# A branch-prefetch hint on VectorE ahead of each slot's choice between two block forms

## The chip, the cores and the metric

The kernel runs on one core of a Trainium2 chip. The metric is device time in microseconds (us) of one execution. The kernel before takes 819.59 us, the median of three runs (819.03, 819.59 and 821.61 us).

## The reference

Three layers follow one another on 3072 tokens of 512 features: a retention attention with a decaying state, and two mixture-of-experts layers in which each token goes to one of eight experts. Cut to the second kind of layer:

```python
e_idx = np.argmax(logits, axis=1)
for e in range(E):                      # E = 8, x: 3072 x 512
    mask = e_idx == e
    h = np.maximum(x[mask] @ w1[e], 0.0)        # 512 -> 1024
    ye = h @ w2[e]                              # 1024 -> 512
    out[mask] = gate_w[mask, None] * eom[mask, e, None] * ye
```

The first expert layer has no `eom`, and adds a per-token bias to its logits. How many tokens go to an expert depends on the data.

## The kernel before

**Tiling.** After the attention the tokens of each expert lie side by side in DRAM. Each expert layer then runs over *slots*: a slot is up to 256 tokens of one expert. Slots 0 to 11 always run (`NSMIN` = 12), up to 19 if the counts ask for it. A slot whose block holds more than 128 tokens is *full* (`run`), one with at most 128 tokens is *small* (`run_small`). Which of the two a slot is, is known only when the tokens have been counted: VectorE writes it as a 0 or 1 into column 7 of the table `meta`, one row per slot, before the layer's slots begin.

**One slot.** `begin` has every engine read the slot's numbers from `meta` into registers (`regs`, lines 832 and 903) and issues the next slot's loads. Then `step` opens `tc.If(s.full > 0)` (line 1146): on each engine the full form stands first, the small form behind it. A full slot falls through the branch at its start and jumps over the small form at its end; a small slot takes the branch at its start.

**Inside a form.** Every product is made in three passes of split numbers (high by high, low by high, high by low). TensorE runs `mm1` (line 922, small: 930), then `mm2` (line 944) in two halves. ScalarE makes the high parts `hh` (912, small: 936) and VectorE the low parts `hl` (913, small: 937). VectorE also splits the next weights when the expert changes (`w1l`, line 506; `w2l`, line 513), turns the next slot's tokens (`xTb`, 542), makes their low part (`xl`, 549), scales the two output halves (`ob`, line 950 in layer 1, 952 in layer 2) and, in layer 1, routes the previous slot's outputs for layer 2 (lines 186 to 260). ScalarE makes the high part of the tokens (`xh`, 547).

**What sets the order.** The schedule is written out by hand: each engine runs its instructions in the order of the code, and waits on semaphores for the others. The code counts quarters of `mm2` with `j`; a full slot has eight (`j` 0 to 7), a small one four.

Of the kernel before, what the change touches and what calls it, by code (L numbers as in the profile page):

```python
# [20 lines left out]
ENG = mybir.EngineType  # L21
# [9 lines left out]
NSMIN, NSL = 12, 19  # L31
# [385 lines left out]
def retention_moe_moe_kernel(ctx: ExitStack, tc: tile.TileContext, q, k, v, mod, mb, wg, wg2, w1, w2, cst_d, out):  # L417
# [90 lines left out]
    def split2(ks=range(KF // 2), parts="hl"):  # L508
        for i in ks:
            if "h" in parts:  # L510
                nc.scalar.activation(w2h[i], raw2[i], AF.Copy)
            if "l" in parts:
                nc.vector.tensor_tensor(w2l[i], raw2[i], w2h[i], op=ALU.subtract)  # L513
# [97 lines left out]
    with ExitStack() as actx:  # L611
# [132 lines left out]
        for i in range(n):  # L744
# [28 lines left out]
            for f in early.get(i, []):  # L773
                f()
            run(*[f() for f in late.get(i, [])])
            if i == 0:
                fetch(3)
# [33 lines left out]
    with ExitStack() as mctx:  # L811
# [19 lines left out]
        def value(at, engines, hi):  # L831
            return nc.values_load(at, engines=engines, min_val=0, max_val=hi, skip_runtime_bounds_check_because=why)
# [7 lines left out]
        class Slot:  # L840
# [167 lines left out]
            def steps(self, steps):  # L1008
                by = {}
                for j, fs in list(steps):  # L1010
                    by.setdefault(j, []).extend(fs)

                def at(j):
                    for f in by.get(j, []):
                        r = f()
                        if hasattr(r, "__next__"):
                            run(r)
                return at
# [22 lines left out]
            def run(self, steps=(), nxt=()):  # L1041

                at, first = self.steps(steps), self.first
                if not first:
                    self.ids()
                    self.split2((0, 1))

                def group(f):
                    at(f)
                    if f == 5:  # L1050
                        self.prepare()
                    if first:
                        for ks, parts in FIRST_W2[self.li - 1].get(f, ()):
                            split2(ks, parts)

                for fs in ((0, 1, 2, 3), (4, 5), (6, 7)):
                    self.mm1(fs, group)
                    for f in fs[1::2]:
                        self.relu(f // 2)
                if first:  # L1060
                    self.ids()
                else:
                    self.split2((2, 3))
                for j in range(8):
                    group(8 + j)
                    if first and j == 5:
                        self.regs()
                        self.load(raw1, w1)
                        self.load(raw2, w2)
                    if first and j == 6:  # L1070
                        self.split1(0)
                    if j == (7 if first else 1):
                        if not first:
                            self.split1(0, "h")
                        self.coming(nxt, Slot.turn)
                        if not first:
                            self.split1(0, "l")
                        self.coming(nxt, Slot.low)
                    if j == (7 if first else 2):
                        self.split1(1)  # L1080
                    self.mm2(j // 4, j % 4)
                    if j % 4 == 3:
                        self.done(j // 4)
                at(16)

            def run_small(self, steps=(), nxt=()):

                at = self.steps(steps)
                self.ids(False)
                one = self.li == 1  # L1090
                if not one:
                    self.split2((0, 1))
                for j in range(4):
                    if j == 3:
                        self.htr(0)
                    at(j)
                    if j == 0 and one:
                        self.split2((0, 1), "h")
                    if j == 1:
                        self.prepare()  # L1100
                    if j > 1:
                        if one:
                            self.split2((j - 2,), "l")
                        self.split2((j,), "h" if one else "hl")
                    self.mm1s(j)
                    if j % 2:
                        nc.scalar.activation(hs[:, (j // 2) * 512:(j // 2 + 1) * 512], hT[j // 2], AF.Relu)
                for j in range(4):
                    if j == 1:
                        self.htr(1)  # L1110
                    at(4 + j)
                    if one and j < 2:
                        self.split2((j + 2,), "l")
                    if j == 1:
                        if self.end:
                            self.load(raw2, w2)
                        self.split1(0, "h")
                        nc.vector.memset(self.o[:, 0, W - 1:], 0.0)
                        if not one:
                            nc.gpsimd.memset(self.o[:, 0, W - 1:], 0.0)  # L1120
                        self.coming(nxt, Slot.turn)
                        self.split1(0, "l")
                        self.coming(nxt, Slot.low)
                    self.mm2(1, j, False)
                self.done(1)
                self.split1(1)
                at(8)
# [5 lines left out]
        def step(li, i, pend=None):  # L1133
            s = Slot(li, i)
            nxt = [Slot(li, i + 1)] if i + 1 < NSL else []
            s.begin(nxt)

            def full():
                s.run(routing(pend, BIG_AT, i >= NSMIN - 2), nxt)

            def small():
                s.run_small(routing(pend, SMALL_AT, i >= NSMIN - 2, hT[2:]), nxt)

            mark = wk.mark()
            before, read = list(pairs), list(reads)
            with tc.If(s.full > 0) as f:  # L1146
                full()
            written, wr = pairs[len(before):], list(reads)
            wk.back(mark)
            pairs[:], reads[:] = before, read  # L1150
            with f.Else():
                small()
            if written:

                pairs[-1] = pairs[-1] + written[-1]
            if reads != wr:
                reads.extend(wr)
            return s

        def routing(pend, at, decide, banks=None):  # L1160
            if pend is None or pend.li == 2:
                return []
            return pend.route(at, decide, banks)[1]
# [20 lines left out]
        def first2(pend):  # L1184
            g, steps = pend.route(FIRST_AT, banks=[xT, hT[3]])
            run(rp2.order())
            first(2, steps[:7], g, FIRST_AT[4], pend.scatter)

        def count(li):
            rp = LAYER[li][0]  # L1190
            return nc.values_load(rp.meta[0:1, 6:7], min_val=NSMIN, max_val=NSL, skip_runtime_bounds_check_because=why)
# [15 lines left out]
        s, n1 = Slot(1, 0), count(1)  # L1207
        for i in range(1, NSMIN):
            s = step(1, i, s)

        def more(i, s):
            if i == NSL:
                return first2(s)
            both(n1 > i, lambda: more(i + 1, step(1, i, s)), lambda: first2(s))
# [4 lines left out]
        for i in range(1, NSMIN):  # L1219
            step(2, i)  # L1220
# [46 lines left out]
```

## Time and profile before

| | before |
|---|---|
| median of the runs | 819.59 us |
| the profiled execution's own time | 813.06 us |
| span of its instructions | 811.3 us |
| TensorE (PE) busy | 780.0 us, 96% |
| VectorE (DVE) busy | 443.1 us, 55% |
| ScalarE (ACT) busy | 263.7 us, 33% |
| GpSimd (POOL) busy | 183.8 us, 23% |
| mean granted TensorE clock | 0.995 |

The profiled execution is one execution, 6.5 us shorter than the median of the timed runs. Register loads, branches and waits are run by an engine's sequencer; they are not counted as busy, and the rows mark them with a q (DVEq). The two expert layers take the time from about 157 us to the end: layer 1's slots 1 to 11 about 157 to 428, layer 2's slots 1 to 11 about 502 to 732.

### The profile page before, as it was taken

The page shows a single profiled execution, that of the slowest core. Times are in us where ns is not written, and L with a number is a line of the kernel's source. Part 1 is how long each engine was busy: PE and PEld are TensorE (multiplying, and loading weights), DVE is VectorE, ACT ScalarE, POOL GpSimd, SP SyncE. Part 2 cuts the span into 40 slices and gives each one's busy share as a digit, 9 for nine tenths or more (in the row PEclk, how much of TensorE's full clock was granted, in tenths as well). Part 3 has the DMA queues.
Part 4 walks back from the last instruction along what each step waited for, and adds up shares of the span by engine and source line. Part 5 has one row for each costly group of instructions (what it writes and reads, how often), then busy time and mean ns, then how long its engine had stood idle before and what let it go on. Part 6 is the DMA issues. An engine that isn't in the chain of part 4 may idle for free. (4 is left out here: it accounts for less than half of the span.)

```text
span 811.3 us, 18995 instructions
## 1 busy us (share of the span) xinstructions
PE 780.0 (96%) x6155; PEld 679.2 (84%) x6155; DVE 443.1 (55%) x1142; ACT 263.7 (33%) x457; POOL 183.8 (23%) x281
## 2 busy tenths in 40 slices
PE   9999998999999999999999978999999999999996
PEld 8888876898888878888889676898888888899784
DVE  5766678833444357435445776235455574553762
ACT  2333345321211244121123441115242552423531
POOL 3456644301110112111001111022211222111131
PEclk9999999999999999999999999999999999999998
DMA  9988999752210117121122435412726277271621
GB/s 184 201 188 212 214 269 320 233 181 55 55 42 15 42 55 242 50 55 54 39 71 68 146 132 152 139 51 73 232 80 200 86 245 229 58 233 41 199 81 58
DMA packets 149741, 107.02 MB, mean 132 GB/s; under 512 B 94893, under 2 KB 125741, under 8 KB 149552
## 3 DMA queue, kind: packets, MB, share of 16 engines
q1 hardware_dynamic: 137616, 85.15, 38.6%
q0 software_dynamic: 6400, 18.98, 6.3%
q10 hardware_dynamic: 5536, 0.75, 0.7%
q8 instruction: 72, 1.18, 0.6%
q14 instruction: 117, 0.96, 0.4%
HBM read 167.64 MB, written 25.83 MB: 238 GB/s over the span
## 5 line engine op out<-in xcount | busy, mean ns | idle before, releaser
L913 DVE SCALAR_TENSOR_TENSOR hl<-hT,hh 128x512 fp32r<-128x512 f32 x96 | 65.3, 689 | 141.8 <-ACT hh L912 98.0
L912 ACT ACTIVATE hh<-hT 128x512 fp32r<-128x512 f32 x96 | 57.3, 598 | 258.3 <-PE hT L922 248.4
L944 PE MATMUL po<-w2h,hl 128*128 128x512 f32 x432 | 125.0, 401 | 0.8 <-DVE hl L913 0.7
L944 PE MATMUL po<-w2l,hh 128*128 128x512 f32 x432 | 118.9, 396 | 1.3 <-DVE w2l L513 1.3
L944 PE MATMUL po<-w2h,hh 128*128 128x512 f32 x432 | 118.7, 396 | 0.0
L922 PE MATMUL hT<-xh,w1h 128*128 128x256 f32 x768 | 106.5, 285 | 10.1 <-ACT xh L547 4.7
L922 PEld LDWEIGHTS hT<-xh,w1h 128*128 128x128 f32 x768 | 97.8, 190 | 16.1 <-ACT xh L547 7.6
L922 PE MATMUL hT<-xl,w1h 128*128 128x256 f32 x768 | 109.4, 283 | 0.3
L922 PE MATMUL hT<-xh,w1l 128*128 128x256 f32 x768 | 101.8, 279 | 0.0
L922 PEld LDWEIGHTS hT<-xl,w1h 128*128 128x128 f32 x768 | 96.8, 188 | 5.8 <-issue 4.5
L944 PEld LDWEIGHTS po<-w2l,hh 128*128 128x128 f32 x432 | 80.8, 188 | 22.2 <-DVE w2l L513 2.2
L922 PEld LDWEIGHTS hT<-xh,w1l 128*128 128x128 f32 x768 | 95.0, 188 | 0.0
L944 PEld LDWEIGHTS po<-w2h,hl 128*128 128x128 f32 x432 | 78.7, 188 | 18.4 <-DVE hl L913 1.1
L944 PEld LDWEIGHTS po<-w2h,hh 128*128 128x128 f32 x432 | 79.3, 188 | 17.2
L954 POOL DMA_INDIRECT out_dram<-ob,to x28 | 42.9, 1532 | 194.7 <-DVE ob L952 108.6
L467 POOL DMA_INDIRECT x2d<-ob,r_idx x28 | 28.8, 1028 | 243.0 <-DVE ob L260 195.1
L547 ACT ACTIVATE xh<-xTb 128x512 fp32r<-128x512 f32 x58 | 33.4, 624 | 81.1 <-DVEq L958 52.4
L513 DVE TENSOR_TENSOR w2l<-raw,w2h 128x1024 fp32r<-128x1024 f32 x44 | 52.4, 1221 | 8.6 <-issue 3.8
L506 DVE TENSOR_TENSOR w1l<-raw,w1h 128x512 fp32r<-128x512 f32 (+1 forms) x84 | 54.3, 706 | 0.0
L542 DVE STREAM_TRANSPOSE xTb<-xqb 128x1024 f32<-128x1024 f32 x29 | 36.1, 1245 | 26.1 <-DMA xmb<-x2d 8.7
L504 ACT ACTIVATE w1h<-raw 128x512 fp32r<-128x512 f32 (+1 forms) x84 | 47.8, 639 | 1.2 <-ACTq L962 0.8
L549 DVE TENSOR_TENSOR xl<-xTb,xh 128x512 fp32r<-128x512 f32 x58 | 37.5, 688 | 15.3 <-ACT xh L547 15.3
(206 smaller groups left out, 928.0 us busy)
## 6 DMA issues: line engine op xcount, KB each, us to landing
raw<-in_w_dram SPq DMA_DIRECT2D x248, 512.0 KB
xqb<-x2d SPq DMA_DIRECT2D x124, 64.0 KB
xqb<-x1d SPq DMA_DIRECT2D x108, 64.0 KB
nq<-in_q_dram SPq DMA_DIRECT2D x24, 256.0 KB
nk<-in_k_dram SPq DMA_DIRECT2D x24, 256.0 KB
nv<-in_v_dram SPq DMA_DIRECT2D x24, 256.0 KB
x1d<-zrow SPq DMA_DIRECT2D x4, 516.0 KB
x2d<-zrow SPq DMA_DIRECT2D x4, 516.0 KB
```

The costliest lines, as they stand in the source:

```text
L467: return nc.gpsimd.indirect_dma_start(out=dst, out_offset=bass.IndirectOffsetOnAxis(ap=rp.idx[:, t:t + 1], axis=0), in_=row, in_offset=Non ...
L504: nc.scalar.activation(w1h[i][:, cols], raw1[i][:, cols], AF.Copy)
L506: los[i].tensor_tensor(w1l[i][:, cols], raw1[i][:, cols], w1h[i][:, cols], op=ALU.subtract)
L513: nc.vector.tensor_tensor(w2l[i], raw2[i], w2h[i], op=ALU.subtract)
L542: nc.vector.transpose(xT.rearrange("p k (a i) -> p a k i", i=32), xq.rearrange("p a (k i) -> p a k i", k=KD))
L547: nc.scalar.activation(hi[:, k:k + 2, :], xT[:, k:k + 2, :], AF.Copy)
L549: nc.vector.tensor_tensor(lo[:, k:k + 2, :], xT[:, k:k + 2, :], hi[:, k:k + 2, :], op=ALU.subtract)
L912: nc.scalar.activation(hh[b], hT[b], AF.Relu)
L913: nc.vector.scalar_tensor_tensor(hl[b], in0=hT[b], scalar=0.0, in1=hh[b], op0=ALU.max, op1=ALU.subtract)
L922: nc.tensor.matmul(hT[f // 2][:, (f % 2) * 2 * P:(f % 2 + 1) * 2 * P], lhsT=a[k][:, f * P:(f + 1) * P], rhs=b[:, k, :], start=(m == 0 and ...
L944: nc.tensor.matmul(po[h], lhsT=x[b][:, o:o + P], rhs=w[f // 2][:, f % 2, :], start=(m == 0 and f == 0), stop=(m == 2 and f == KF - 1))
L954: nc.gpsimd.indirect_dma_start(out=out, out_offset=bass.IndirectOffsetOnAxis(ap=to[:, t:t + 1], axis=0), in_=o[:, :DM], in_offset=None, bo ...
```

## The change

```diff
@@ run (full form)
                 for j in range(8):
                     group(8 + j)
+                    if j == 6 and not first:
+                        self.hint()
...
+            def hint(self):
+                i = self.i + 1
+                if not self.end and i < NSL and (self.li == 1 or i < NSMIN):
+                    full = value(self.rp.meta[i:i + 1, 7:8], [ENG.DVE], 1)
+                    tc.mark_branch_hint_location(f"s{self.li}_{i}", hint=full, engines=[ENG.DVE])
@@ run_small
                 for j in range(4):
+                    if j == 2:
+                        self.hint()
...
@@ step
-            with tc.If(s.full > 0) as f:
+            with tc.If(s.full > 0, label=f"s{li}_{i}") as f:
```

`hint` has VectorE read the next slot's column 7 into a register and puts a hint instruction there, which is tied by its label to that slot's branch. By its interface a register value of 0 (the next slot is small) asks for the instructions at the branch's target, a value of 1 (full) for none. By the conditions in `hint` and `not first`, the hints stand in slots 1 to 10 of each layer and speak of slots 2 to 11. Each stands in both forms: 40 pairs in the program, of which an execution runs 20. The instruction rows of TensorE are as many as before (8552), VectorE's go from 4753 to 4833.

The first place is VectorE in the full form of layer 1's slot 1, between the two scalings of the output (`po_120` is the first half's bank; `rR` and `r_base` are the routing's ranks). In pieces of the difference + is the change:

```order
 L958 UNCONDITIONAL_BRANCH x2
 L950 TENSOR_SCALAR ob_2270<-po_120,xmb_2267 128x4x4x32
+L832 TENSOR_LOAD r_meta
+L1272 BRANCH_PREFETCH_HINT
 L221 TENSOR_TENSOR rR_720<-misc,r_base 128x24
 L222 COPY r_base<-rR_720 128x8
```

The load and the hint come in behind the first half's scaling and ahead of the rank sum, which waits for TensorE; nothing else moved. (Line 1272 is the end of the program's context, where hints are filled in.)

The second place is VectorE in the small form of layer 2's slot 1, behind the low part of the next tokens; the first fence is the kernel before:

```order
L958 UNCONDITIONAL_BRANCH x2
L549 TENSOR_TENSOR xl<-xTb,xh 128x512 x2
L952 TENSOR_SCALAR ob_2270<-po_121,xmb_2267 128x512
L958 COMPARE_AND_BRANCH
L506 TENSOR_TENSOR w1l_96<-raw_84,w1h_92 128x512
```

and this is the change:

```order
L958 UNCONDITIONAL_BRANCH x2
L549 TENSOR_TENSOR xl<-xTb,xh 128x512 x2
L832 TENSOR_LOAD r_meta
L1272 BRANCH_PREFETCH_HINT
L952 TENSOR_SCALAR ob_2270<-po_121,xmb_2267 128x512
L958 COMPARE_AND_BRANCH
L506 TENSOR_TENSOR w1l_96<-raw_84,w1h_92 128x512
```

Here the pair stands ahead of the output's scaling and of the second half of the next expert's `w1l` (line 506, behind the branch of line 958). Between the hint and the branch it speaks of stands that other branch.

## Rows read from the trace of the kernel before

**Rows 1.** The page's first part: busy time, share of the span, instructions.
```profile
PE 780.0 (96%) x6155; PEld 679.2 (84%) x6155; DVE 443.1 (55%) x1142; ACT 263.7 (33%) x457; POOL 183.8 (23%) x281
```

**Rows 2.** Stretches: length, busy PE, PEld, DVE, ACT, POOL, clock, DMA share, GB/s.
```profile
264.00:288.00 24.00, 24.00 (x158) 20.77 (x157) 10.02 (x32) 4.87 (x10) 3.29 (x7) 1.00 0.12 36
288.00:309.00 21.00, 19.86 (x126) 16.23 (x125) 12.38 (x39) 12.46 (x22) 2.86 (x7) 1.00 0.28 83
...
549.00:564.00 15.00, 14.97 (x79) 12.40 (x78) 7.35 (x12) 8.34 (x15) 1.86 (x6) 1.00 0.23 55
...
629.00:644.00 15.00, 14.60 (x74) 11.74 (x73) 6.60 (x11) 7.58 (x14) 1.85 (x6) 1.00 0.23 61
644.00:665.00 21.00, 20.90 (x130) 18.51 (x131) 16.64 (x24) 13.04 (x21) 6.93 (x5) 1.00 0.66 215
```

**Rows 3.** Line 1146 (a slot's branches) by engine: count, ns min/median/max, first and last start.
```profile
L1146 PEldq COMPARE_BRANCH  x50: 65/171/3782, 159.2 to 788.2; - x50
...
L1146 DVEq COMPARE_BRANCH  x50: 43/47/69, 164.2 to 793.4; - x50
```

**Rows 4.** Line 832 (register loads) on VectorE, same columns; then two in a row.
```profile
L832 DVEq TENSOR_LOAD <-r_meta x61: 299/310/558, 157.2 to 792.6; - x61
...
L832 DVEq TENSOR_LOAD <-r_meta x2: 304/307/310, 263.4 to 263.7; - x2
```

**Rows 5.** VectorE, branch not taken (full slot at 264.5), and the next sequencer row.
```profile
L1146 DVEq COMPARE_BRANCH  x1: 55/55/55, 264.5 to 264.5; - x1
...
L962 DVEq COMPARE_BRANCH  x1: 63/63/63, 264.6 to 264.6; - x1
```

**Rows 6.** VectorE, branch taken: first and last of three hinted small slots, next row behind.
```profile
L1146 DVEq COMPARE_BRANCH  x1: 56/56/56, 289.2 to 289.2; - x1
...
L962 DVEq COMPARE_BRANCH  x1: 56/56/56, 289.7 to 289.7; - x1
...
L1146 DVEq COMPARE_BRANCH  x1: 56/56/56, 630.5 to 630.5; - x1
...
L962 DVEq COMPARE_BRANCH  x1: 56/56/56, 631.0 to 631.0; - x1
```

**Rows 7.** VectorE, a jump far ahead at layer 1's end, and its first instruction there.
```profile
L1146 DVEq COMPARE_BRANCH  x1: 69/69/69, 455.0 to 455.0; - x1
...
L272 DVE TENSOR_TENSOR sct<-r_base,cst x1: 167/167/167, 457.2 to 457.2; 128x8 f32<-128x8 f32 x1
```

**Rows 8.** VectorE in order of time, full slot to full slot: start, us, instruction, [idle before].
```profile
256.72 0.75 DVE L950 TENSOR_SCALAR ob<-po,xmb 128x512 f32<-128x512 f32 x1 [0.22 <-DVEq L958]
259.89 0.18 DVE L221 TENSOR_TENSOR rR<-misc,r_base 128x24 f32<-128x24 f32 x1 [2.41 <-PE misc L217]
...
266.96 1.50 DVE L913 SCALAR_TENSOR_TENSOR hl<-hT,hh 128x512 fp32r<-128x512 f32 x2 [3.64 <-ACT hh L912]
```

**Rows 9.** VectorE, then TensorE, in the small slot at 289 and behind it.
```profile
290.42 0.42 DVE L983 COPY lT<-misc 128x256 f32<-128x256 f32 x1 [2.42 <-issue]
293.04 0.69 DVE L937 TENSOR_TENSOR hl<-hT,hh 128x512 fp32r<-128x512 f32 x1 [2.19 <-ACTq L962]
296.72 0.69 DVE L937 TENSOR_TENSOR hl<-hT,hh 128x512 fp32r<-128x512 f32 x1 [2.44 <-ACT hh L936]
...
289.64 0.64 PE L981 MATMUL misc<-oT,wgp 128*32 128x256 f32 x8
...
301.40 1.85 PE L922 MATMUL hT<-xh,w1h 128*128 128x256 f32 x11 [1.02 <-ACT xh L547]
```

**Rows 10.** VectorE, then TensorE, from layer 2's small slot 3 into slot 4.
```profile
562.33 1.29 DVE L549 TENSOR_TENSOR xl<-xTb,xh 128x512 fp32r<-128x512 f32 x2
563.54 0.75 DVE L952 TENSOR_SCALAR ob<-po,xmb 128x512 f32<-128x512 f32 x1
564.20 2.49 DVE L506 TENSOR_TENSOR w1l<-raw,w1h 128x512 fp32r<-128x512 f32 x4
...
569.21 1.10 PE L922 MATMUL hT<-xh,w1l 128*128 128x256 f32 x8
```

## The prediction, made before the changed kernel was run

> **What bounds the kernel.** I read the page's first part, then busy time by stretch cut at the slots, then the branch rows, then VectorE's rows in order of time. TensorE is busy 780.0 us of the span of 811.3 us, VectorE 443.1 us [rows 1]. The reader should see that an instruction on VectorE costs time only if TensorE ends up waiting for it. The hinted stretch, slots 2 to 11 of each layer, is 20 slots; cut at their edges (190 to 428 and 528 to 732 us), 16 of the 20 stretches have no idle TensorE at all, like the one at 264, and the other four have 1.14, 0.03, 0.40 and 0.10 us [rows 2], together **1.67 us**. That is all the time that any speed-up of VectorE could give back there.
>
> **What the change adds.** 20 register loads run. A load takes 0.31 us in the middle of its rows, and of two in a row the second starts 0.3 to 0.4 us behind the first [rows 4]; I count 0.4 us, so 20 x 0.4 = 8 us of VectorE's sequencer. 20 hints run, and the trace before has none. From below, a hint is worth what a branch row takes, 0.04 us [rows 3]; from above, if the sequencer stands still until the fetch has come, the longest branch of all, 3.78 us on TensorE's own sequencer [rows 3]. I take 0.05 us, since the hint asks and doesn't jump, which is nearest to the VectorE branch of 0.047 us. Sum: 20 x 0.45 = 9 us of VectorE's sequencer, at most 84 us by the upper end.
>
> What hides it. In a full slot the pair stands behind the first half's scaling. That one runs from 256.72 to 257.47, and VectorE then idles 2.41 us until TensorE's rank sum is there [rows 8]: 0.45 fits five times. In layer 2, which has no routing, the next row on VectorE is the scaling of the second half, which waits for TensorE's `mm2` as well. Behind the pair, the next slot's first `hl` comes after a further idle 3.64 us, waiting for ScalarE [rows 8], so a late VectorE is late for nobody. If these covers were gone the loss would be the 9 us less what idles later in the slot.
>
> In a small slot the pair stands ahead of the second half's scaling and of the next expert's `w1l`, and here VectorE is full: 562.33 to 566.69 without a gap [rows 10]. Three of the 20 are of this kind. `w1l`'s four pieces end at 564.20 + 2.49 = 566.69, and TensorE takes them at 569.21 [rows 10]: **2.5 us** of slack against 0.45. Cost on TensorE: nothing.
>
> **What the change removes.** Only a taken branch can gain. In the hinted slots VectorE takes three (the small slots at 289, 551 and 630 us). From the branch to the next sequencer row a taken one needs 0.5 us (289.2 to 289.7, 630.5 to 631.0) [rows 6], one that is not taken 0.1 us [rows 5]. At best 3 x 0.4 = 1.2 us of VectorE goes; at worst nothing, if the 0.4 us is the jump itself. I take 0.4 us each as possible and none of it on the path. In the slot at 289 the first VectorE work is the copy `lT` at 290.42, which needs the product of TensorE that runs from 289.64 to 290.28 [rows 9]. Behind it VectorE waits twice more, 2.19 and 2.44 us, for ScalarE and through it for TensorE [rows 9], and only then comes the chain to the tokens' high part for which TensorE idles 1.02 us at 301.40 [rows 9]. Time saved at 289.2 can't pass those waits. So even the largest of the four idle spots stays.
>
> The new labels and the moved addresses change no row of the other engines. VectorE's program is 80 rows longer, so its blocks of code shift; jumps that needed 0.5 us can become shorter and others longer, inside the same slack.
>
> **The sum.** Of the profiled execution's own 813.06 us: added 0, removed 0, so 813.1. That execution is 6.5 us below the median of the timed runs, 819.59; a change of zero carries over as it stands: **819.6 us**. The three runs shown lie from 819.03 to 821.61, which is 0.3% of the time, about what a measurement of this kernel can tell from no change.
>
> **A rule weighed.** A jump that leaves the near code does cost on this engine: at layer 1's end, from the branch at 455.0 to the first instruction at 457.2, it is 2.2 us [rows 7]. The slot branches at 0.5 us are not of that kind. [...]
>
> **Rivals.**
>
> *Faster.* The hint shortens the start of the small slots and, through moved code, other jumps, and TensorE's idle time after small slots goes. For it: three of the four idle stretches hold or follow a small slot. Against it: the two waits of [rows 9]. Its price is bounded by the 1.67 us, so it gives 819.59 - 1.67 = 817.9 us at the very best, which is still inside 0.3%. Beyond 0.3% there is only what I don't see. Chance of over 0.3%: 0.05.
>
> *Slower: the hint takes VectorE's code away or holds its sequencer.* Place: the three small slots, where VectorE is full up to the next slot's `w1l`. If a hint holds the sequencer as long as the longest branch row, 3.78 + 0.4 = 4.2 us, then `w1l` comes 4.2 - 2.5 = 1.7 us late [rows 3, 10], three times: 5 us, 824.6 us. If the next jump must fetch as well, 2.2 us more each [rows 7], it is 3 x 3.9 = 11.6 us, 831 us. It decides from a hold of 2.5 us on. For it: the row of 3.78 us exists. Against it: that is TensorE's sequencer at a real jump, no VectorE slot branch is above 0.07 us [rows 3], and these three slots are followed by full ones, for which the hint asks for no fetch. [...] Worked from rows, a loss of 2.2 us in each of the 20 slots is 44 us of VectorE, of which only 2.2 + 0.45 - 2.5 = 0.15 us in each of three small slots reaches TensorE, 0.5 us in all: 820.1 us, no change. Chance of slower by over 0.3%: 0.08.
>
> *The change doesn't do what it says.* Between the hint and its branch VectorE passes another jump: over the small form at a full slot's end, and in a small slot the branch of line 958. If that jump uses up or drops the hint, the taken branches stay at 0.5 us and only the 9 us of hidden sequencer time remain: 819.6 us, the same number as the forecast. Chance 0.25, which lies inside "same".
>
> **How the numbers follow.** Hidden either way (the hint works or is dropped): 0.87 for within 0.3%, of which 0.25 is the dropped hint. Faster by more: 0.05. Slower by more: 0.08. The range reaches down past the full 1.67 us (817.9) and up past the highest of the three runs (821.61): **817.6 to 822.0 us**. It leaves out the long hold at 824.6 and above. The upper end of a hint's cost, 3.78 us, is kept in the range only as far as the slack takes it.
>
> **What would show it.** VectorE's line of register loads should go from 61 to 81 rows, and 20 hint rows appear with some 0.05 us each. Next to the branches at the three small slots the following row should come 0.1 to 0.5 us later: nearer 0.1 if the hint works, still 0.5 if it is dropped. TensorE's busy time should stay at 780 us, and its idle time in the 20 stretches at 1 to 3 us. A hint row of over 2.5 us, a VectorE sequencer gap of 2 us behind a slot's jump, or new TensorE waits for `w1l` or `hl` in slots 2 to 11 would prove the forecast wrong, and so would TensorE idle time vanishing after the small slots.

## The result and the profile after

The change is **slower by 0.64%**: 822.32 us against 819.19 us, ratio 1.0064 with a 95% interval of 1.004 to 1.0087, which is 5.2 us of 819. The ratio is an estimate from the runs and not the quotient of the two medians, which lie 3.1 us (0.4%) apart: the runs of before spread from 812.89 to 821.61 us. Measured again further down, the change is 0.56% slower and the medians lie 4.0 us apart. The profiled execution after took 821.4 us, with a span of 819.6 us. That of before, at 813.06 us, lay 6 us under its median, so the two traces stand further apart (8.3 us of span) than the runs.

| | before | after |
|---|---|---|
| median of the runs | 819.19 us | 822.32 us |
| PE busy | 780.0 us | 784.4 us |
| DVE busy | 443.1 us | 443.1 us |
| mean granted TensorE clock | 0.995 | 0.993 |

What was added is as small as forecast. Line by line on VectorE after (its lines lie 10 further on; line 1156 is the slots' branch): count, ns min/median/max, first and last start.

```profile
L1156 DVEq COMPARE_BRANCH  x50: 43/50/88, 165.3 to 802.4; - x50
...
L832 DVEq TENSOR_LOAD <-r_meta x81: 299/309/545, 158.2 to 801.6; - x81
...
L1272 DVEq BRANCH_PREFETCH_HINT  x20: 34/34/52, 184.0 to 714.4; - x20
```

20 loads more than in [rows 4], 20 hints of 0.034 us, branches about as short as in [rows 3]. The time is lost elsewhere. The hinted stretches of layer 1 and layer 2, first of the kernel before, then after: length, busy PE, PEld, DVE, ACT, POOL, clock, DMA share, GB/s.

```profile
189.00:428.00 239.00, 237.87 (x1588) 207.68 (x1587) 110.69 (x359) 56.69 (x102) 34.01 (x70) 1.00 0.23 66
528.00:732.00 204.00, 203.47 (x1257) 180.44 (x1256) 110.18 (x147) 75.72 (x120) 41.08 (x61) 1.00 0.47 148
```

```profile
190.00:431.00 241.00, 237.96 (x1585) 207.29 (x1584) 110.54 (x359) 56.72 (x102) 33.56 (x70) 1.00 0.23 65
...
533.00:740.00 207.00, 204.43 (x1261) 180.83 (x1261) 110.61 (x148) 75.72 (x120) 40.58 (x61) 1.00 0.46 146
```

TensorE's idle time goes from 1.13 + 0.53 = 1.66 us to 3.04 + 2.57 = 5.61 us: **4 us more**, which is most of the loss. The added time sits at two places. TensorE after, in order of time: start, us, instruction, [idle before <- what ended it].

```profile
302.81 2.43 PE L922 MATMUL hT<-xh,w1h 128*128 128x256 f32 x16 [1.02 <-ACT xh L547]
307.02 2.16 PE L922 MATMUL hT<-xl,w1h 128*128 128x256 f32 x13 [1.79 <-DVE xl L549]
...
569.15 2.07 PE L922 MATMUL hT<-xh,w1h 128*128 128x256 f32 x13 [1.87 <-ACT xh L547]
```

The 1.02 us stood there before [rows 9]; the 1.79 us and the 1.87 us are new. Both come behind a small slot (slot 6 of layer 1, slot 3 of layer 2), and both wait for the next slot's tokens, `xl` and `xh`. Behind the third hinted small slot (slot 7 of layer 2) nothing of the kind is added. VectorE at these places, first before, then after:

```profile
299.07 0.06 DVE L1118 MEMSET ob<- 128x1 f32 x1 [0.46 <-DVEq L962]
299.38 1.25 DVE L542 STREAM_TRANSPOSE xTb<-xqb 128x1024 f32<-128x1024 f32 x1 [0.25 <-issue]
300.55 1.25 DVE L506 TENSOR_TENSOR w1l<-raw,w1h 128x512 fp32r<-128x512 f32 x2
...
558.73 0.06 DVE L1118 MEMSET ob<- 128x1 f32 x1
558.79 1.25 DVE L542 STREAM_TRANSPOSE xTb<-xqb 128x1024 f32<-128x1024 f32 x1
```

```profile
300.78 1.25 DVE L542 STREAM_TRANSPOSE xTb<-xqb 128x1024 f32<-128x1024 f32 x1 [0.25 <-issue]
303.87 1.29 DVE L506 TENSOR_TENSOR w1l<-raw,w1h 128x512 fp32r<-128x512 f32 x2 [1.84 <-ACT w1h L504]
...
564.45 0.06 DVE L1128 MEMSET ob<- 128x1 f32 x1
567.13 1.25 DVE L542 STREAM_TRANSPOSE xTb<-xqb 128x1024 f32<-128x1024 f32 x1 [2.62 <-issue]
```

Before, the transpose follows the fill at once and `w1l` the transpose. After, VectorE stops for 1.84 us and 2.62 us in the middle of the small form. Its sequencer shows the same: in slot 6 nothing between a branch and the wait ahead of `w1l`. VectorE's sequencer, lines 958 and 506 after:

```profile
L958 DVEq COMPARE_BRANCH  x3: 43/47/50, 300.2 to 300.8; - x3
...
L506 DVEq EVENT_SEMAPHORE  x1: 21/21/21, 303.8 to 303.8; - x1
```

That is 300.8 to 303.8, 3 us. The releaser named (ScalarE's `w1h`) is the latest one in the profile, not the cause. Its first four pieces end at 299.54 + 2.20 = 301.74, 2 us ahead of the wait's end, and before, `w1l` started at 300.55 on these four (the fifth began at 301.77). ScalarE after:

```profile
299.54 2.20 ACT L504 ACTIVATE w1h<-raw 128x512 fp32r<-128x512 f32 x4
```

The second stop is put down to "issue". What each stop does hold is a packet of instructions. The instruction queue q14 before, in the stretches 289.1:301 and 551:564: packets, MB, share.

```profile
q14 instruction: 2, 0.02, 0.3%
...
q14 instruction: 3, 0.02, 0.6%
```

And after, in the stretches 290.8:304, 300.9:304 and 564.5:567 (290.8:301 and 556.7:564.5 have none of q14):

```profile
q14 instruction: 1, 0.01, 0.1%
...
q14 instruction: 1, 0.01, 0.6%
...
q14 instruction: 1, 0.01, 1.2%
```

Before, packets of q14 come in the same part of the slot without a stop; after, the only one of slot 6 that comes later than 0.3 us behind the branch lies in the stop, and in slot 3 none comes in the 7.8 us ahead of the stop. The view doesn't say for which engine a packet is, so that these are VectorE's is inferred from the time.

The packets inside both stops, one of 0.01 MB each, fit a sequencer that waits for its code. That is the author's reading; no view shows what the sequencer waits for.

### The profile page after: what moved, and what is told of

Read it like the earlier page. It is cut to its first block, busy times and chain, and to the rows that moved or that the text cites. A ratio compares the mean times of both kernels' runs of the same rounds, so it can differ in the third digit from the quotient of the medians.

```text
span 819.6 us, 19035 instructions
## 1 busy us (share of the span) xinstructions
PE 784.4 (96%) x6155; PEld 682.7 (83%) x6155; DVE 443.1 (54%) x1142; ACT 263.9 (32%) x457; POOL 181.5 (22%) x281
```

## The experiments

Theory 1: behind a hinted branch that is taken, the code that follows isn't there in time, and VectorE stops in the small form until it is fetched. Theory 2: the 80 rows moved VectorE's code to a worse place. Theory 3: the loads and hints cost by themselves. Each ratio is to the kernel before on the same chip.

**The change again.**

> The change as it is, beside the next three on the same chip. Three theories. (1) Displaced code: when a hinted branch is taken, VectorE's next stretch of code is no longer brought in ahead, and it stops 2 to 3 us in the small form of a hinted small slot (3.0 us at 300.8 and 2.4 us at 564.5 us in the trace of the change). (2) Moved code: the 80 more instructions move the borders at which code is fetched, and the stops come from there. (3) The pairs themselves cost: 20 loads and hints on VectorE's queue. All three: 1.004 to 1.009 of the kernel before, with two stops of over 2 us inside small slots 6 of layer 1 and 3 of layer 2.

820.47 us, ratio 1.0056 (1.0034 to 1.0079). Stops of 2.77 and 2.42 us at the same places, TensorE idle 1.62 and 1.87 us behind them.

**Fills in place of hints (theory 2).**

```diff
-                    full = value(self.rp.meta[i:i + 1, 7:8], [ENG.DVE], 1)
-                    tc.mark_branch_hint_location(f"s{self.li}_{i}", hint=full, engines=[ENG.DVE])
+                    nc.vector.memset(filler, 0.0)
+                    nc.vector.memset(filler, 0.0)
```

> In place of each pair two memsets of one column: VectorE's program is as long as the change's, each later instruction stands where it stands there, but nothing is hinted. (1) Displaced code: no stop of over 1 us inside the three small slots, 0.998 to 1.002 of before. (2) Moved code: the same two stops as in the change at the same instructions, 1.004 to 1.009. (3) Pairs' own cost: no stops, under 1.002.

816.4 us, ratio 0.9989 (0.9964 to 1.0015). Ahead of layer 2 VectorE executes as many waits here as in the change (215), behind it 10 fewer (158 against 168), so in layer 2 the positions aren't the same to the row. VectorE in slot 6 without a hint, at the same place in the program:

```profile
304.63 0.06 DVE L1129 MEMSET ob<- 128x1 f32 x1 [0.46 <-DVEq L963]
304.94 1.25 DVE L542 STREAM_TRANSPOSE xTb<-xqb 128x1024 f32<-128x1024 f32 x1 [0.25 <-issue]
306.11 2.45 DVE L506 TENSOR_TENSOR w1l<-raw,w1h 128x512 fp32r<-128x512 f32 x4
```

No stop (0.25 us of idle time), and none in slot 3 of layer 2, where the transpose starts with the fill at 562.89. Theory 2 falls for this position: moved code without hints costs nothing that can be measured there (ratio 0.9989). A second thing shows here. The branch into slot 6, and the next row (line 1156 and 962 after; 1157 and 963 here):

```profile
L1156 DVEq COMPARE_BRANCH  x1: 75/75/75, 290.5 to 290.5; - x1
...
L962 DVEq COMPARE_BRANCH  x1: 71/71/71, 290.7 to 290.7; - x1
```

```profile
L1157 DVEq COMPARE_BRANCH  x1: 56/56/56, 294.7 to 294.7; - x1
...
L963 DVEq COMPARE_BRANCH  x1: 56/56/56, 295.0 to 295.0; - x1
```

0.2 us with a hint, 0.2 to 0.3 us without one. The 0.5 us of [rows 6] went with the moved code; the hint gained nothing at this jump. At the third small slot the same step takes 0.6 us with the hint and 0.2 us without.

**All hints ask for nothing (theory 3).**

```diff
+        always = mk.tile([P, 1], I32, name="always")
+        nc.gpsimd.memset(always, 1)
...
-                    full = value(self.rp.meta[i:i + 1, 7:8], [ENG.DVE], 1)
+                    full = value(always[0:1, 0:1], [ENG.DVE], 1)
```

> The pairs stay, but the load reads a constant 1, so each hint asks for nothing. (1) Displaced code: no code is fetched by a hint, so no stops in the small slots, 0.998 to 1.002 of before. (2) Moved code: the two stops stay, 1.004 to 1.009. (3) Pairs' own cost: all of the cost stays, 1.004 to 1.009, without stops.

814.82 us, ratio 0.9979 (0.9957 to 1.0). All 20 loads and hints run, no stop (0.63 us of idle time ahead of slot 6's transpose): theory 3 falls. What is left are the three hints that ask for code, of which two lead to a stop.

**All hints ask for the small form**: the same with `memset(always, 0)`, so that 17 of 20 are wrong.

> The pairs stay, but the load reads a constant 0, so all 20 hints ask for the small form, 17 of them wrongly. (1) Displaced code: stops of 2 to 3 us in the three small slots as in the change, and further ones in full slots, where VectorE has 2.5 us and more to spare: 1.005 to 1.02 of before. (2) Moved code: the same as the change, 1.004 to 1.009, with no further stops. (3) Pairs' own cost: the same as the change.

824.7 us, ratio 1.0091 (1.0069 to 1.0112). This program and the last one differ in one constant, so no position of code differs between them: that the hints which ask for code make the loss is shown here best. The two stops stay, and some full slots stop at the jump over their small form: VectorE's slot branch, then the next slot's first load (here lines 1158 and 834).

```profile
L1158 DVEq COMPARE_BRANCH  x1: 79/79/79, 217.2 to 217.2; - x1
...
L834 DVEq TENSOR_LOAD <-r_meta x2: 306/312/317, 220.4 to 220.8; - x2
```

217.2 to 220.4 is 3.2 us (two more, of 2.8 and 2.9 us, at 410 and 699; the other full slots have none). TensorE has no idle time there: in a full slot the cover that the prediction named holds even 3 us. Still the kernel takes 4.2 us more than the change on the same chip. A part of this is slot 6, where the stop stands ahead of the transpose here and TensorE idles 3.87 us at one place, against 1.02 + 1.62 us there:

```profile
308.23 2.17 PE L924 MATMUL hT<-xh,w1h 128*128 128x256 f32 x8 [3.87 <-ACT xh L547]
```

The rest wasn't placed, so what the wrong hints cost in all stays open.

**The hint at the small form's start.**

```diff
                 at = self.steps(steps)
+                self.hint()
...
-                    if j == 2:
-                        self.hint()
```

> The change, with the pair of the small form moved from its last quarter to its start, so ahead of the two stops instead of behind them. There it speaks of the next slot, which is full after each of the three small slots, so the hint asks for nothing. (1a) A hint that asks for nothing lets VectorE's code come in ahead again: the two stops of over 2 us go, 0.998 to 1.002 of before. (1b) Once the hinted branch is taken nothing brings it back until VectorE reaches the border: the stops stay, 1.004 to 1.009.

822.95 us, ratio 1.0072 (1.0046 to 1.0097). Both stops stay, 2.91 and 2.22 us. They come two sequencer rows earlier than in the change, in slot 6 ahead of the transpose instead of behind it: just the load and the hint that now stand in front. TensorE then idles 3.87 us in slot 6, as in the run before.

```profile
299.54 0.06 DVE L1127 MEMSET ob<- 128x1 f32 x1 [0.45 <-DVEq L962]
302.71 1.25 DVE L542 STREAM_TRANSPOSE xTb<-xqb 128x1024 f32<-128x1024 f32 x1 [3.11 <-issue]
```

So here a hint that asks for nothing didn't remove the stop, and the stop wasn't tied to a row's data.

**A hint where a jump is long.** In the kernel before, TensorE's branch at layer 1's end takes 5.24 us and leaves it idle for 4.69 us. Here VectorE gets no hint, and TensorE one for that branch.

```diff
+            def far(self):
+                if self.end and self.i + 1 < NSL:
+                    on = value(self.rp.meta[self.i:self.i + 1, 5:6], [ENG.PE], 1)
+                    tc.mark_branch_hint_location(f"m{self.i + 1}", hint=on, engines=[ENG.PE])
...
-            with tc.If(c) as f:
+            with tc.If(c, label=label) as f:
```

> The kernel before without any hint on VectorE, with one on TensorE's sequencer instead: in the last quarter of layer 1's slots 11 to 17 it asks for the target of the branch to layer 2 (line 1196) where no further slot comes. That branch holds TensorE's sequencer 5.2 us in the trace of before, and TensorE idles 4.7 us behind it. (1) If a hinted branch finds its code there, the idle time at layer 1's end falls from 4.7 us to under 2 us, but at TensorE's next border of code there may be a stop of up to 3 us: 0.995 to 1.000 of before. If the hint does nothing on TensorE: 0.999 to 1.001, with 4.7 us of idle time.

814.03 us, ratio 0.995 (0.9931 to 0.9969): a gain of 0.5% on the kernel before. The branch on TensorE's sequencer, in the kernel before and with the hint:

```profile
L1196 PEldq COMPARE_BRANCH  x1: 5242/5242/5242, 467.2 to 467.2; - x1
```

```profile
L1205 PEldq COMPARE_BRANCH  x1: 366/366/366, 467.5 to 467.5; - x1
```

And TensorE's first products behind it, again before and with the hint:

```profile
472.57 2.68 PE L922 MATMUL hT<-xh,w1h 128*128 128x256 f32 x11 [4.69 <-ACT w1h L504]
```

```profile
469.53 1.64 PE L922 MATMUL hT<-xh,w1h 128*128 128x256 f32 x10 [1.26 <-ACT xh L547]
```

5.24 us of branch became 0.37 us, 4.69 us of idle time 1.26 us. The branch takes 3.3 to 6.6 us in all thirteen traces without this hint and 0.37 to 0.38 us in the three with it. But the thirteen add no rows to TensorE's code, the hint does, and no run has fills on TensorE in its place: that the hint and not the moved code does it is likely, but not shown. About 12 us later TensorE waits for VectorE's `lT`, where it had no wait before:

```profile
482.00 0.67 PE L988 MATMUL misc<-cst,lT 128*128 128x16 f32 x4 [2.09 <-DVE lT L983]
```

So of the 3.4 us won at the jump 2.1 us are given back, and what makes up the whole 0.5% isn't shown.

**The same with a second hint behind the jump**, which asks for nothing.

> As the run before, with a second hint on TensorE at the start of the target that asks for nothing (its register holds 1). (1a) A hint that asks for nothing lets the code come in ahead again: no stop behind the jump, 0.993 to 0.998 of before. (1b) It brings nothing back: as the run before.

812.37 us, ratio 0.9946 (0.9924 to 0.9968), the same 1.26 us. The second hint does nothing that can be seen.

**The stop and the position.** Rows that never run (slot 1 is full in both layers) move all VectorE code behind them:

```diff
             def run_small(self, steps=(), nxt=()):
+                if self.li == 1 and self.i == 1:
+                    for k in range(16):
+                        nc.vector.memset(filler, 0.0)
```

> The change, with 16 VectorE rows more in the small form of slot 1, which never runs in this data, so that all later VectorE code lies 16 rows further on. Theory 1 (VectorE runs into a code border that nobody has fetched): the border stays where it is in memory, so both stops of 2 to 3 us come 16 rows earlier in the program. In slot 6 of layer 1 that is in the routing rows near 299 us, from which to the tokens' low part VectorE has no idle time, so TensorE still waits 1.8 us or more there; the ratio stays at 1.004 to 1.008. Rival (the stop belongs to the rows at which it was seen, a wait for data or a semaphore): the stops stay in front of the same rows, ratio 1.006.

821.65 us, ratio 1.0077 (1.0049 to 1.0106). In slot 6 the stop (2.96 us) now comes nine executed rows earlier, behind the routing, and TensorE idles 1.63 and 1.94 us. There are branches among the nine rows, so how many rows of the program they span the trace doesn't say. In layer 2's slot 3 it did not move: it stands ahead of the same wait as in the change. So a fixed border in memory is at best half right: the position counts, but the rule for where the stop falls isn't found.

The same with `range(40)`:

> As before with 40 rows in place of 16. Theory 1: in slot 6 of layer 1 the border falls some 40 rows earlier, between the two sums of the hidden low part, where VectorE idles about 2 us for ScalarE, so the stop is there and TensorE does not wait for the tokens; in slot 3 of layer 2 the border falls ahead of the small form, in code that is jumped over, so that stop is gone. Ratio 0.998 to 1.003, if no other border comes to lie in a tight place (slot 7 of layer 2 is the one that could). Rival (the stop belongs to its rows): nothing moves, ratio 1.006.

809.01 us, ratio **0.9929** (0.9896 to 0.9962): no loss, but a gain that was not expected. The long stop in slot 6 has moved right behind the slot's branch (branch, then next row; lines 1160 and 963 here):

```profile
L1160 DVEq COMPARE_BRANCH  x1: 75/75/75, 288.7 to 288.7; - x1
...
L963 DVEq COMPARE_BRANCH  x1: 71/71/71, 290.4 to 290.4; - x1
```

1.7 us where VectorE has slack [rows 9]; TensorE behind it idles the old 1.02 us, and slot 3 of layer 2 has no stop.

The kernel before with the 16 and with the 40 rows, without hints:

> The kernel before, without hints, with the same 16 rows in the small form of slot 1: what moved code alone does. Theory 1: behind a taken branch without a hint the following page is fetched in time wherever the border lies, so no stop of 2 us in a small slot and a ratio of 0.997 to 1.002. Rival (code position decides, not the hint): stops as in the change, ratio 1.004 or more.

813.22 us, ratio 0.9976 (0.9953 to 0.9998).

> The kernel before, without hints, with 40 rows in the small form of slot 1 that never runs: how much of the gain of the change with 40 rows is the moved code alone. Theory 1: no stop of 2 us in the small slots either way, so what remains is the layers' border, where the change with 40 rows had no stop behind the slot branch near 457 us and a shorter one ahead of slot 1 of layer 2; if that comes from the position alone, the ratio is 0.993 to 0.996; if the hints in their own right give part of it, 0.997 to 1.0.

816.04 us, ratio 0.9999 (0.9969 to 1.0029). No stop in the small slots in either.

**40 rows and TensorE's hint together.**

> The change with the 40 rows and with the hint for TensorE at layer 1's far branch, which took the idle time there from 4.7 to 1.2 us when it was put into the kernel before. With the 40 rows 2.8 us of idle time are left at that place, so the hint takes up to 1.6 us more: ratio 0.990 to 0.993 if the two gains add, 0.993 or above if the hint's gain is lost behind VectorE's own late start in layer 2.

809.14 us, ratio 0.9915 (0.9879 to 0.9951), not told apart from the 40 rows alone. TensorE without and with its own hint:

```profile
468.14 2.09 PE L923 MATMUL hT<-xh,w1h 128*128 128x256 f32 x14 [2.84 <-ACT w1h L504]
...
479.01 0.62 PE L989 MATMUL misc<-cst,lT 128*128 128x16 f32 x4 [0.39 <-DVE lT L984]
```

```profile
466.57 0.81 PE L923 MATMUL hT<-xh,w1h 128*128 128x256 f32 x3 [1.25 <-ACT xh L547]
...
479.02 0.62 PE L989 MATMUL misc<-cst,lT 128*128 128x16 f32 x4 [2.10 <-DVE lT L984]
```

1.6 us won at the jump, and all of it given back at VectorE's `lT`, for which TensorE starts at 479 us either way.

**Position or hints?** The 40 rows, with fills in place of the hints; then the 40 rows with hints once more.

> The kernel with the 40 rows, each pair of load and hint replaced by two small fills, so that every VectorE row stands at the place in memory where the hinted kernel has it, and none is a hint. If the position of the code at the layers' border gives the gain: no stop behind the slot branch near 454 us either, TensorE without the wait of 1.8 to 2.0 us for the routing's transpose there, ratio 0.992 to 0.995. If the hints give it (the jump at layer 1's end, or the small slots): the stop of 3.7 us is there, ratio 0.998 to 1.002.

811.02 us, ratio 0.9953 (0.9926 to 0.9979).

> The change with the 40 rows once more, for the comparison on one chip: 0.993 again, from 0.990 to 0.996.

807.48 us, ratio **0.9895** (0.9865 to 0.9925), the fastest of all. So the fills alone give about 0.5% here and the hints about as much again; the two intervals just don't overlap. As in the first fills run VectorE executes 10 waits fewer in layer 2 than with the hints (158 against 168), and no run with the 40 rows has hints that ask for nothing, so that the hints make the second half is argued and not shown. The traces differ at two far jumps of VectorE that no hint speaks of. Without hints, slot branch and first row at layer 1's end, then branch and first load ahead of layer 2's slots:

```profile
L1160 DVEq COMPARE_BRANCH  x1: 69/69/69, 454.2 to 454.2; - x1
...
L272 DVE TENSOR_TENSOR sct<-r_base,cst x1: 168/168/168, 455.5 to 455.5; 128x8 f32<-128x8 f32 x1
...
L1210 DVEq COMPARE_BRANCH  x1: 47/47/47, 500.7 to 500.7; - x1
...
L1205 DVEq TENSOR_LOAD <-r_meta x1: 312/312/312, 507.1 to 507.1; - x1
```

With hints (the first run with 40 rows):

```profile
L1160 DVEq COMPARE_BRANCH  x1: 69/69/69, 454.0 to 454.0; - x1
...
L272 DVE TENSOR_TENSOR sct<-r_base,cst x1: 166/166/166, 454.2 to 454.2; 128x8 f32<-128x8 f32 x1
...
L1210 DVEq COMPARE_BRANCH  x1: 53/53/53, 500.4 to 500.4; - x1
...
L1205 DVEq TENSOR_LOAD <-r_meta x1: 311/311/311, 502.7 to 502.7; - x1
```

1.3 against 0.2 us and 6.4 against 2.3 us. The second jump took 2.3 to 2.8 us in all three hinted runs with 40 rows and 5.5 to 6.4 us in the other runs, the hinted ones among them. TensorE's idle time from slot 12 of layer 1 to slot 1 of layer 2 is 9.3 us without the hints and 7.0 and 8.0 us with them, 1.3 to 2.3 of the 3.5 us between the two medians. Why the jumps differ, and whether they give all of the 0.5%, stays open.

**All traces together.** Cut at the ends of slots 1 and 11 of each layer, TensorE idles 5.3 to 7.0 us in the hinted stretches in the five traces that have both stops, and 1.3 to 2.7 us in the eleven that don't.

## Why the prediction was wrong

Forecast 819.6 us with a range up to 822.0; measured 822.32, and slower by 0.64% where "slower" had a chance of 0.08.

**What bounds the kernel, and what was added**: right. TensorE bounds it; loads and hints are 20 of each, at 0.31 and 0.034 us, and cost nothing by themselves (0.9979 with all of them in place, asking for nothing).

**What hides it**: right for the full slots, where even 3.2 us are covered.

**The failed step** is the sum's "added 0", from "Cost on TensorE: nothing" in the small slots: it counts the pairs' own 0.45 us and nothing that a hint does later. That came in only as the rival "the hint takes VectorE's code away", at 0.08: right that a hint brings a loss later (stops of 2.2 to 3.0 us), wrong in its place and so in its price; that code was taken away is not shown. The prediction set the fetch at the hint or at the jump behind it, and gave it the 2.5 us of slack that `w1l` has [rows 10]; by that it cost 0.15 us in each small slot. It looked at the hints that stand in small slots, which ask for nothing as the next slot is full. The three that ask for code stand in the full slots ahead, and the stop came behind their branch, among the small form's rows around `xTb`, ahead of the rest of `w1l` and `xl`. There the path runs `xTb`, ScalarE's `xh`, TensorE. In layer 2's slot 3 before, ScalarE and TensorE:

```profile
560.13 1.16 ACT L547 ACTIVATE xh<-xTb 128x512 fp32r<-128x512 f32 x2
...
561.39 1.80 PE L922 MATMUL hT<-xh,w1h 128*128 128x256 f32 x14
```

The first half of `xh` is there at 560.13 + 1.16/2 = 560.7, TensorE starts at 561.39: 0.7 us of slack. A stop of 2.62 us makes 1.9 us of idle time, and 1.87 was measured. In slot 6 there is hardly any: [rows 9] shows TensorE idle for `xh` already. The transpose still ran (300.78 to 302.03) while the sequencer stood (300.8 to 303.8), so 3 us of stop took 1.84 us from VectorE and made 1.79 us of idle time at `xl`. Twice 1.8 us is most of the loss. The rest wasn't placed: between the two stretches TensorE idles no longer after (10.4 us from 431 to 533) than before (10.8 us from 428 to 528), and its busy time, 4.4 us longer in the trace after, is 3.9 us longer also in that of the first fills run, which is no slower than before. At the third small slot VectorE idles 1.21 us ahead of its transpose, against 1.13 us before: no such stop, and why this hinted branch has none stays open.

**"No VectorE slot branch is above 0.07 us"** was an argument from a trace without hints, which couldn't show what comes behind one; it should have raised the upper bound at the tightest place instead. The rival's name, "takes VectorE's code away", pointed at a loss behind the hint, and its price was worked out for one place only.

**What the change removes**: right that none of it is on the path, wrong in what it is. The 0.5 us of a near taken branch is also 0.2 us without a hint at the same place in the program, so hints removed nothing there. (All four idle stretches hold or follow a small slot, not three as the rival "faster" says.)

**The hint is dropped**: false. Hints act: the stops came with hints that ask for code (ratio 1.0091 with all 20 of them) and not with 20 that ask for nothing (0.9979).

## What to carry to other kernels

Bound a stop of unknown place at the spot where the chain to the bottleneck has the least slack, not where the new instruction stands. A hint is worth trying where a jump is long and the bottleneck waits for it: with one, TensorE's branch of 5.24 us took 0.37 us and the kernel 0.995 of its time, and of the 3.4 us won 2.1 us went to the wait for the next engine, VectorE. At VectorE's jumps of 0.2 to 0.5 us hints gave nothing. When code moves, run a twin with the same rows and no hints, or, closer still, the same hints with a constant that makes them ask for nothing: fills alone moved this kernel by 0.5%, and the same hints cost 0.6% at one position and stood 0.6% below their fills at another.

## What the hardware showed

- Behind two of three hinted branches that are taken, VectorE's sequencer stopped for 2.2 to 3.0 us, 14 to 33 executed rows into the small form; with 40 rows more one stop moved right behind the branch (1.3 to 1.7 us) and the other went. With 20 hints that ask for nothing it did not (0.63 us of idle time at the first place). The one packet of 0.01 MB inside each stop fits a wait for code, which is the author's reading and not shown; what decides where the stop falls, and why the third branch has none, is open.
- With hints that name the wrong side VectorE stopped for 2.8 to 3.2 us at the next jump in three of the full slots, and not in the others.
- With a hint TensorE's branch at layer 1's end took 0.37 us in place of 5.24 us (3.3 to 6.6 us in all traces without it); the moved code wasn't tested apart. On VectorE, jumps with no hint of their own became shorter in the hinted kernel with 40 rows (6.4 to 2.3 us).
